# Transposes of q and x: from TensorE to the DMA crossbar on the SyncE queue

## The chip, the cores and the metric

The kernel runs on one core of a Trainium2 chip. The metric is the device time of one execution in microseconds (us). Ratios are the mean time of one kernel's fast runs over the mean of the other's fast runs of the same rounds, so they are not quite the ratio of the medians that stand beside them.

Engine names as in the profile: PE is TensorE (matmuls), PEld its weight loads, DVE is VectorE, ACT is ScalarE, POOL is GpSimd, SP is SyncE. L271 is line 271 of the kernel in question; the changed kernel is 25 lines longer from line 265 on, so L286, L331, L275 of the kernel before are L311, L356, L300 of the changed one.

## The reference

Linear attention followed by a gated feed-forward layer, for 8 batches of 576 tokens, 8 heads of 64.

```python
def _attn_ref(q, k, v, g_norm):
    kv = np.einsum('bhsd,bhse->bhde', k, v)
    out = np.einsum('bhsd,bhde->bhse', q, kv)
    rms = np.sqrt(np.mean(out * out, axis=-1, keepdims=True) + 1e-06)
    return (out / rms * g_norm).astype(np.float32)

def _moe_ref(x, w_gate, w_val, w_out, w_res):      # x: 4608 x 512
    g = x @ w_gate                                  # 512 x 1536
    gelu = 0.5 * g * (1.0 + erf(g * inv_sqrt2))
    val = x @ w_val
    ffn_out = gelu * val @ w_out
    res_gate = 1.0 / (1.0 + np.exp(-(x @ w_res)))
    return (x + res_gate * ffn_out).astype(np.float32)
```

## The kernel before

Each batch has 512 main tokens, a block of its own, and 64 remainder tokens. The remainders of all batches form a ninth block; the remainder rows of two batches are worked on together with the odd one of the pair. The feed-forward part of block b runs on TensorE while the attention of batch b+1 is put between its pieces ("slots"): twelve slots of one gate and one value chain (4 + 4 matmuls of 128x512), then four slots of one residual chain and one output chain (4 + 12 matmuls).

TensorE transposes q (for q times kv) and the normalised x (for the feed-forward part); ACT carries both from PSUM to SBUF, x with the scale g_norm:

```python
def a_qT(b, jj):
    q16 = b16_t[b, "q"].rearrange("p j h d -> p j (h d)")
    ps = pattn.tile([P, 2, NP, P], FP16, tag="at", name="qtp")
    for e in range(2):
        for pr in range(NP):
            nc.tensor.transpose(ps[:, e, pr, :], q16[:, 2 * jj + e, pr * P : (pr + 1) * P], ident)
    nc.scalar.copy(out=st[b]["qT"][:, 2 * jj : 2 * jj + 2, :, :], in_=ps)

def a_xT(b, j):
    ...                                              # cut
    for cc in range(NP):
        nc.tensor.transpose(ps[:, cc, :], t_t[blk][:, jj, cc * P : (cc + 1) * P], ident)
    nc.scalar.activation(out=xT_t[blk][:, :, jj * P : (jj + 1) * P], in_=ps, func=AF.Copy, scale=gcol)

def a_x(b, j):                                       # t*g, for the residual only
    nc.vector.tensor_tensor(out=t_t[blk][:, jj, :], in0=t_t[blk][:, jj, :], in1=g16, op=ALU.mult)
```

The product that closes a slot on DVE, and the chain that reads it:

```python
def m_act(blk, f, gps, vps):
    ge = moep.tile([P, NJ * P], FP16, tag="ge", name="ge")
    nc.scalar.activation(out=ge, in_=gps, func=AF.Gelu)
    nc.vector.tensor_tensor(out=hids[blk][:, f, :], in0=ge, in1=vps, op=ALU.mult)      # hid f
...
    nc.tensor.matmul(fps, lhsT=hids[blk][:, f, j * P : (j + 1) * P], rhs=wo16[:, f, :], ...)
```

The attention plan, one list per slot of the block before (o: q times kv; t: normalised out; x: a_xT; y: a_x):

```python
[by_token q, by_token k],                       # DVE casts q and k to token order
[attn_begin, a_qT(b, 0), load_batch(b + 1)],    # loads of the next batch, issued by POOL
[a_qT(b, 1), a_kv(b, 0, 2)],
[a_kv(b, 2, 4)] + ([a_rem_qT(b)] if odd),
[o[0]] + ([a_rem_o(b)] if odd), [o[1]], [o[2]], [o[3]],
[a_norm(b), t[0], t[1]],                        # slot 8
[t[2], t[3]],
[t[4]] if odd, [],
[x[0], x[1]], [x[2], x[3], y[0], y[1]], [x[4] if odd, y[2], y[3]], [y[4]] if odd
```

(lambdas and slices cut.)

## Time and profile before

| | kernel before |
|---|---|
| time, median of 3 runs | 376.47 us (375.27 to 376.87) |
| span of the profiled run | 373.6 us, granted clock 0.993 |
| PE busy | 358.0 us, 96% |
| a block of the feed-forward part with attention in it (first residual chain of one block to that of the next, 89.06 to 128.14 us) | 39.1 us |

Two more groups of PE work, kept apart by shape, matter later. Columns: line, engine, operation, out<-in, shapes, count; busy us and mean ns; idle time of PE just before them.

```profile
L331 PE MATMUL fps<-wo,hid 128*128 128x512 f16 x432 | 99.6, 379 | 0.0
...
L190 PE MATMUL op<-kv,qT 128*128 128x128 f16 x112 | 10.8, 219 | 0.0
```

PE never stands idle ahead of the output chain (fps) or of q times kv (op): both last columns are 0.0. Those columns show first whether a change has put a wait there.

### The profile page before, as it was taken

To read this page: it belongs to the slowest core of one execution; us is meant where nothing else is said; L and a number is where in the kernel's file an instruction comes from. 1 tells how busy PE (TensorE), PEld (TensorE's weight loads), DVE (VectorE), ACT (ScalarE), POOL (GpSimd) and SP (SyncE) were. 2 spreads that over 40 slices of the span, in tenths; PEclk is the share of its full clock that TensorE was granted. 3 is DMA by queue.
4 is the path that set the end of the run, shared out by engine and by line. 5 is a ranking of instruction groups with operands and counts; after the bars stand their busy time and mean duration, and the time that the engine had idled before them with its cause. 6 is when DMAs were issued, how large, how long until landed. Compare 5 with 4: busy or idle time off the path is not lost.

```text
span 373.6 us, 5442 instructions
## 1 busy us (share of the span) xinstructions
PE 358.0 (96%) x2120; PEld 180.6 (48%) x2120; DVE 215.6 (58%) x427; ACT 153.2 (41%) x257; POOL 47.0 (13%) x65
## 2 busy tenths in 40 slices
PE   6779999999999999999999999999999999999993
PEld 2554464554455455545464445444644444444441
DVE  2566448778546946584657664756478453343422
ACT  3563373453346344544364335533563333123310
POOL 3843140500050002200130005000000000000000
PEclk9899999999999999999999999999999999999998
DMA  9999997590159012901192029601000200020013
GB/s 246 187 202 197 198 200 74 81 221 2 58 107 141 0 56 63 182 5 56 61 172 18 28 84 133 58 31 56 30 0 2 84 29 2 28 80 7 0 43 70
DMA packets 49452, 30.76 MB, mean 82 GB/s; under 512 B 14098, under 2 KB 44818, under 8 KB 49426
## 3 DMA queue, kind: packets, MB, share of 16 engines
q0 software_dynamic: 40848, 17.83, 38.2%
q1 hardware_dynamic: 8578, 12.59, 9.6%
q8 instruction: 16, 0.26, 0.3%
q14 instruction: 10, 0.08, 0.1%
HBM read 38.80 MB, written 9.44 MB: 129 GB/s over the span
## 4 chain that ended last, share of the span: by engine, by line
PE 90%; DVE 5%; DMA 2%; ACT 1%; issue 1%; SPq 0%; DVEq 0%
PE gps L286 25%; PE vps L286 24%; PE fps L331 24%; PE rps L318 8%; DMA qf<-in_q_dram 2%; PE xtp L260 2%; PE kvp L161 2%; PE qtp L151 2%; PE op L190 2%; DVE t L501 1%; DVE pf L337 1%; DVE ss L485 1%; ACT xT L521 1%; PE orp L208 0%; PE kvp L168 0%
## 5 line engine op out<-in xcount | busy, mean ns | idle before, releaser
L286 PE MATMUL gps<-xT,wg 128*128 128x512 f16 (+1 forms) x456 | 112.6, 368 | 2.0 <-ACT xT L521 1.5
L275 DVE TENSOR_TENSOR hid<-ge,vps 128x512 f16<-128x512 f16 x108 | 73.6, 685 | 68.0 <-PE vps L286 67.8
L286 PE MATMUL vps<-xT,wv 128*128 128x512 f16 (+1 forms) x456 | 111.9, 368 | 0.0
L274 ACT ACTIVATE ge<-gps 128x512 f16<-128x512 f32 x108 | 64.5, 598 | 99.7 <-PE gps L286 92.9
L331 PE MATMUL fps<-wo,hid 128*128 128x512 f16 x432 | 99.6, 379 | 0.0
L286 PEld LDWEIGHTS <-wv 128*128 128x128 f16 x456 | 43.6, 98 | 50.2 <-issue 0.2
L331 PEld LDWEIGHTS <-hid 128*128 128x128 f16 x432 | 42.0, 98 | 49.3
L286 PEld LDWEIGHTS <-wg 128*128 128x128 f16 x456 | 41.8, 98 | 42.7 <-issue 2.6
L337 DVE SCALAR_TENSOR_TENSOR pf<-th,fps 128x512 f32<-128x512 f32 x36 | 24.5, 688 | 59.4 <-PE fps L331 59.4
L318 PE MATMUL rps<-wr,xT 128*128 128x512 f16 x144 | 36.9, 379 | 0.1
L327 ACT ACTIVATE th<-rps 128x512 f32<-128x512 f32 x36 | 21.5, 598 | 37.7 <-PE rps L318 37.7
L261 ACT ACTIVATE xT<-xtp,gcol 128x512 f16<-128x512 f16 x32 | 20.5, 685 | 37.6 <-PE xtp L260 37.6
L99 POOL DMA_DIRECT2D qraw<-in_q_dram x7 | 6.3, 894 | 162.0 <-DVE q L106 126.8
L342 DVE SCALAR_TENSOR_TENSOR osb<-pf,t 128x512 f32<-128x512 f32 x36 | 24.9, 691 | 1.1
L184 DVE TENSOR_REDUCE ss<-sq 128x8 f32<-128x512 f32 x32 | 21.9, 686 | 5.5 <-ACT sq L183 3.0
L183 ACT ACTIVATE sq<-op 128x512 f32<-128x512 f32 x28 | 16.8, 598 | 12.0 <-PE op L190 12.0
L318 PEld LDWEIGHTS <-xT 128*128 128x128 f16 x144 | 13.2, 98 | 13.9 <-issue 1.5
L248 DVE TENSOR_TENSOR t<-op,ny 128x512 f16<-128x512 f32 x28 | 17.9, 683 | 0.3
L152 ACT COPY qT<-qtp 128x1024 f16<-128x1024 f16 x14 | 14.2, 1013 | 9.1 <-PE qtp L151 9.1
L161 PE MATMUL kvp<-v,k 128*128 128x128 f16 x128 | 10.9, 222 | 3.3 <-POOL v L434 2.2
L267 DVE TENSOR_TENSOR t<-t,g 128x512 f16<-128x512 f16 x36 | 13.5, 418 | 0.0
L190 PEld LDWEIGHTS <-qT 128*128 128x128 f16 x112 | 8.6, 98 | 6.6
(82 smaller groups left out, 203.4 us busy)
## 6 DMA issues: line engine op xcount, KB each, us to landing
out_dram<-osb SPq DMA_DIRECT2D x32, 256.0 KB, 2.3
qraw<-in_q_dram POOLq DMA_DIRECT2D x7, 512.0 KB, 6.0
kraw<-in_k_dram POOLq DMA_DIRECT2D x7, 512.0 KB, 7.9
v<-in_v_dram POOLq DMA_DIRECT2D x7, 512.0 KB, 9.8
wo<-in_moe_w_out_dram POOLq DMA_DIRECT2D x3, 512.0 KB, 13.8
qf<-in_q_dram SPq DMA_DIRECT2D x2, 512.0 KB, 7.6
kf<-in_k_dram SPq DMA_DIRECT2D x2, 512.0 KB, 6.5
vf<-in_v_dram SPq DMA_DIRECT2D x2, 512.0 KB, 7.8
```

Of the source, the lines that this page charges most:

```text
L161: nc.tensor.matmul(ps, lhsT=k16[:, j, cs], rhs=v16[:, 2 * pr : 2 * pr + 2, j * D : (j + 1) * D], start=(j == 0), stop=False,)
L184: nc.vector.tensor_reduce(out=st[b]["ss"][:, j, :], in_=sq, op=ALU.add, axis=mybir.AxisListType.X)
L248: nc.vector.tensor_tensor(out=t_t[blk][:, jj, :].rearrange("p (h d) -> p h d", h=H), in0=s["o"][j].rearrange("p (h d) -> p h d", h=H), in1 ...
L261: nc.scalar.activation(out=xT_t[blk][:, :, jj * P : (jj + 1) * P], in_=ps, func=AF.Copy, scale=gcol)
L274: nc.scalar.activation(out=ge, in_=gps, func=AF.Gelu)
L275: nc.vector.tensor_tensor(out=hids[blk][:, f, :], in0=ge, in1=vps, op=ALU.mult)
L286: nc.tensor.matmul(ps[:, j0 * P : j1 * P], lhsT=w[:, cc, :], rhs=xT_t[blk][:, cc, j0 * P : j1 * P], start=(cc == 0), stop=(cc == NP - 1),)
L318: nc.tensor.matmul(rps, lhsT=xT_t[blk][:, cc, j * P : (j + 1) * P], rhs=wr16[:, cc, :], start=(cc == 0), stop=(cc == NP - 1),)
L327: nc.scalar.activation(out=th, in_=rps, func=AF.Tanh, scale=0.5)
L331: nc.tensor.matmul(fps, lhsT=hids[blk][:, f, j * P : (j + 1) * P], rhs=wo16[:, f, :], start=(f == 0), stop=(f == NF - 1))
L337: nc.vector.scalar_tensor_tensor(out=pf, in0=th, scalar=1.0, in1=fps, op0=ALU.add, op1=ALU.mult)
L342: nc.vector.scalar_tensor_tensor(out=osb, in0=pf, scalar=0.5, in1=t_t[blk][:, j, :], op0=ALU.mult, op1=ALU.add)
```

## The change

The intent: PE is the bound, so take transposes off it. For batches 2 to 7 the DMA queue of SyncE transposes q (and, in odd batches, the remainder of q) and x from SBUF to SBUF. ACT's copy applied the scale g_norm; the transposing DMA in this kernel carries no scale, so DVE multiplies x with g_norm beforehand. xT is laid out chunk by chunk, so that one DMA can write several of its chunks. As q's transpose takes longer, q times kv and what follows move to one slot later.

```diff
-        xT_t[blk] = pool.tile([P, NP, NJ * P], FP16, ...)
+        xT_t[blk] = pool.tile([P, NJ, NP, P], FP16, ...)
+    def d_qT(b):
+        nc.sync.dma_start(
+            out=st[b]["qT"].rearrange("p j c t -> p (j c) t"),
+            in_=b16_t[b, "q"].rearrange("p j h d -> p (j h d)"),
+            transpose=True,
+        )
+    def d_rem_qT(b):
+        st[b]["qrT"] = attnp.tile([P, NP, P], FP16, tag="qrT", name="qrT")
+        nc.sync.dma_start(out=st[b]["qrT"], in_=qr_t[b // 2], transpose=True)
+    def rem_qT_copy(b):
+        nc.scalar.copy(out=qtr[0][:, :, 0:R], in_=st[b]["qrT"][:, :, 0:R])
+        ...                                          # cut: the other half
+    def d_xT(b, j0, j1):
+        nc.sync.dma_start(out=xT_t[blk][:, k0:k1, :, :]..., in_=t_t[blk][:, k0:k1, :]..., transpose=True)
-                rhs=xT_t[blk][:, cc, j0 * P : j1 * P],
+                rhs=xT_t[blk][:, j0:j1, cc, :],
+    def attn_plan_dma(b):                            # for batches 2 to 7; lambdas cut
+            [by_token q, by_token k],
+            [attn_begin, d_qT(b)] + ([d_rem_qT(b)] if odd) + [load_batch(b + 1)],
+            [a_kv(b, 0, 2)], [a_kv(b, 2, 4)],
+            [rem_qT_copy(b)] if odd,
+            [o[0]] + ([a_rem_o(b)] if odd), [o[1]], [o[2]], [o[3]],
+            [a_norm(b), t[0], t[1], y[0], y[1], d_xT(b, 0, 2)],      # slot 9
+            [t[2], t[3], y[2], y[3], d_xT(b, 2, 4)],
+            [t[4], y[4], d_xT(b, 4, 5)] if odd,
```

(Other places that follow the new layout are cut.)

More of the change, by code (lines that the diff above doesn't have):

```diff
@@ L134, in new_block @@
         t_t[blk] = pool.tile([P, NJ, C], FP16, tag="t" if blk < B else "tl", name="t")
-        xT_t[blk] = pool.tile([P, NP, NJ * P], FP16, tag="xT" if blk < B else "xTl", name="xT")
+        xT_t[blk] = pool.tile([P, NJ, NP, P], FP16, tag="xT" if blk < B else "xTl", name="xT")
     def attn_begin(b):
@@ L261, in a_xT @@
         nc.scalar.activation(
-            out=xT_t[blk][:, :, jj * P : (jj + 1) * P], in_=ps, func=AF.Copy, scale=gcol
+            out=xT_t[blk][:, jj, :, :], in_=ps, func=AF.Copy, scale=gcol
         )
@@ L267, in a_x @@
         nc.vector.tensor_tensor(out=t_t[blk][:, jj, :], in0=t_t[blk][:, jj, :], in1=g16, op=ALU.mult)
+    def d_qT(b):
[9 more added lines that the diff above has]
+        nc.scalar.copy(out=qtr[0][:, :, 0:R], in_=st[b]["qrT"][:, :, 0:R])
+        nc.scalar.copy(out=qtr[1][:, :, R : 2 * R], in_=st[b]["qrT"][:, :, R : 2 * R])
+    def d_xT(b, j0, j1):
+        blk, k0 = where(b, j0)
+        k1 = k0 + j1 - j0
+        nc.sync.dma_start(
+            out=xT_t[blk][:, k0:k1, :, :].rearrange("p j c t -> p (j c) t"),
+            in_=t_t[blk][:, k0:k1, :].rearrange("p j c -> p (j c)"),
+            transpose=True,
+        )
     hids = {}
@@ L319, in m_res @@
                 rps,
-                lhsT=xT_t[blk][:, cc, j * P : (j + 1) * P],
+                lhsT=xT_t[blk][:, j, cc, :],
                 rhs=wr16[:, cc, :],
@@ L516, in f_xT_out @@
         ps = first["xT", half, j0]
-        dst = xT0[:, 2 * half : 2 * half + 2, j0 * P : (j0 + n) * P].rearrange("p c (j t) -> p c j t", j=n)
+        dst = xT0[:, j0 : j0 + n, 2 * half : 2 * half + 2, :].rearrange("p j c t -> p c j t")
         if on_vector:
@@ L631, in attn_plan @@
         ]
+    def attn_plan_dma(b):
+        odd = b % 2 == 1
+        o = [lambda j=j: a_o(b, j) for j in range(NJ)]
+        t = [lambda j=j: a_t(b, j) for j in range(NJ + 1)]
+        y = [lambda j=j: a_x(b, j) for j in range(NJ + 1)]
+        return [
+            [lambda: by_token(b, "q"), lambda: by_token(b, "k")],
+            [lambda: attn_begin(b), lambda: d_qT(b)]
+            + ([lambda: d_rem_qT(b)] if odd else [])
+            + ([lambda: load_batch(b + 1)] if b + 1 < B else []),
+            [lambda: a_kv(b, 0, 2)],
+            [lambda: a_kv(b, 2, 4)],
+            [lambda: rem_qT_copy(b)] if odd else [],
+            [o[0]] + ([lambda: a_rem_o(b)] if odd else []),
+            [o[1]],
+            [o[2]],
+            [o[3]],
+            [lambda: a_norm(b), t[0], t[1], y[0], y[1], lambda: d_xT(b, 0, 2)],
+            [t[2], t[3], y[2], y[3], lambda: d_xT(b, 2, 4)],
+            [t[4], y[4], lambda: d_xT(b, 4, 5)] if odd else [],
+        ]
     late = []
@@ L650 @@
             new_block(blk + 1)
-            for i, fs in enumerate(attn_plan(blk + 1)):
+            for i, fs in enumerate((attn_plan if blk == 0 else attn_plan_dma)(blk + 1)):
                 plan.setdefault((NF - 1 if blk == 0 else 0) + i, []).extend(fs)
```

## The prediction

> **What bounds the kernel now.** I read the page first, its busy times and the chain of waits:
>
> ```profile
> PE 358.0 (96%) x2120; PEld 180.6 (48%) x2120; DVE 215.6 (58%) x427; ACT 153.2 (41%) x257; POOL 47.0 (13%) x65
> ...
> PE 90%; DVE 5%; DMA 2%; ACT 1%; issue 1%; SPq 0%; DVEq 0%
> ```
>
> TensorE (PE) is busy 358.0 of 373.6 us, and 90% of the chain that ends last is PE. So PE time removed shortens the span, unless another engine then makes PE wait. The groups of PE instructions kept apart by shape show what the change can remove:
>
> ```profile
> L260 PE MATMUL xtp<-ident,t 128*128 128x128 f16 x128 | 10.3, 219 | 0.6 <-DVE t L248 0.6
> L151 PE MATMUL qtp<-ident,q 128*128 128x128 f16 x112 | 8.6, 219 | 0.6 <-DVE q L106 0.6
> L200 PE MATMUL qtrp<-ident,qr 128*128 128x128 f16 x16 | 1.5, 219 | 0.0
> ```
>
> The 219 ns is the latency of one transpose; pipelined ones follow faster. The timeline of the block that starts at 103.69 us (block 2, which prepares batch 3) gives the pitch: eight q transposes start at 107.14 and the next gate matmul starts at 107.59, so 56 ns each. Twelve 128x512 matmuls of a chain piece take 2.59 us, so 216 ns each.
>
> The third view is the same timeline where VectorE (DVE) closes the gate/value part (columns: start, length, engine, line):
>
> ```profile
> 121.07 1.03 PE L286 MATMUL gps<-xT,wg 128*128 128x512 f16 x4
> ...
> 123.07 0.69 DVE L275 TENSOR_TENSOR hid<-ge,vps 128x512 f16<-128x512 f16 x1 [0.48 <-PE vps L286]
> ...
> 123.68 0.18 DVE L230 TENSOR_SCALAR nm<-ss 128x40 f32<-128x40 f32 x1
> ...
> 126.21 1.29 DVE L248 TENSOR_TENSOR t<-op,ny 128x512 f16<-128x512 f32 x2
> ...
> 127.41 0.68 DVE L275 TENSOR_TENSOR hid<-ge,vps 128x512 f16<-128x512 f16 x1
> ...
> 128.01 1.28 DVE L248 TENSOR_TENSOR t<-op,ny 128x512 f16<-128x512 f32 x2
> ...
> 129.00 2.75 PE L331 MATMUL fps<-wo,hid 128*128 128x512 f16 x12
> ...
> 129.80 0.68 DVE L248 TENSOR_TENSOR t<-o,ny 128x512 f16<-128x512 f32 x1
> 130.40 0.68 DVE L275 TENSOR_TENSOR hid<-ge,vps 128x512 f16<-128x512 f16 x1
> ```
>
> These hid products are those of slots 8, 9, 10 and 11, the last four of twelve; between them stand the normalisation (nm to ny) and the products t. The first output matmul chain (fps) reads hid of slot 11 only in its twelfth matmul, due at 129.00 + 11 x 0.216 = 131.38. That hid ends at 130.40 + 0.68 = 131.08. So DVE is 58% busy over all, but here it has only 0.3 us of slack before PE would wait.
>
> **What the Trainium skill says.** (1) "VectorE: DVE Perf Modes", section "The three transpose paths": 390 ns for a 128x128 transpose on TensorE, 1309 ns through the DMA crossbar. The trace has 219 ns latency and 56 ns pitch, so on PE a transpose costs less than the page says. (2) "Advanced Engine Details and Errata", section "X-Bar Transpose (TRN2)": transposing DMAs run at 350 to 400 GB/s. The trace of the kernel before has none. (3) "DMA: Bandwidth & Descriptors", section "Anatomy of one DMA": about 2.0 us fixed per DMA. This is given for the software path, but the 256 KB output stores, issued by SyncE, landing in 2.3 us, fit it. (4) The same page, section "Issuing engines are not separate DMA queues": all queues share the 16 DMA engines. In the trace the loads of the next batch fill these from 109.8 to 118.3 us, just when a q transpose would run.
>
> **The change part by part.** *Removed from PE:* for batches 2 to 7, 16 q and 16 x transposes each, and in batches 3, 5, 7 four more of each for the remainder rows: 6 x 32 + 3 x 8 = 216. At 56 ns: 12.1 us, all on the path. That alone would be 3.2% of 376.47. *Removed from ScalarE (ACT):* 12 qT copies at 1.01 us and 27 scaled xT copies at 0.69 us, some 31 us, but ACT is 41% busy and waits for PE: worth nothing by itself. *New xT layout:* the gate/value matmuls now read four runs of 128 columns. The matmuls of k and v already read two runs of 64 columns at 222 ns against 219 for others, so I count it as free.
>
> *Moved on DVE, which I hold for the main point.* The order of instructions in the changed kernel shows the normalisation one slot later (after hid 9, not hid 8), and the products t*g, formerly done near the end of the block, now between hid 9, hid 10 and hid 11. Count from T, the start of slot 9's gate matmuls. In the trace the slot 8 hid starts 2.00 after its slot's start (123.07 - 121.07) and the norm 2.61 after. The norm takes 2.53 (123.68 to 126.21), each t or hid 0.60 (pitch in the rows above), a pair of t*g about 0.67 (two ran in 0.75 at the block's end, overlap taken off). So norm from T+2.61; two t from T+5.14; two t*g from T+6.34; hid 10 from T+7.01; two t from T+7.61; two t*g from T+8.81; hid 11 from T+9.48 to T+10.16. PE: three slots of eight matmuls at 0.216 (5.19), four rps (0.86), eleven fps (2.38): it wants hid 11 at T+8.43. **PE waits 1.73 us**, with the restart some 1.8, in each of six blocks: 10.8 us. hid 10 is ready at T+7.69, in time for the tenth product's turn at T+8.21. So the twelve us removed come nearly all back as one wait per block.
>
> *Added on the DMA queue.* One transpose of 128x2048 f16 (512 KB) for q per batch, two of 256 KB for x, and 128 KB for each remainder. For x: t*g of the second pair ends at T+9.5, and the next block begins at about T+5.19 + 4 x 3.46 + 1.8 = T+20.8, so it has 11 us: hidden. For q: its cast ended at 106.98, that is 3.3 us into the block. The first o matmul now comes after six slots and 20 k-v matmuls: 6 x 1.73 + 20 x 0.056 = 11.5 us. **The budget is 8.2 us.** Estimate: 2.0 fixed and 0.52 MB at 350 GB/s 1.5 make 3.5 us alone. But it splits into short rows, shares the engines with the loads from about 2.8 us after its start, and the 1309 ns of the page for one 128x128 block, times 16 blocks one after another, would be 21 us. I choose 8.5 us as the middle, wide: a wait of 0.3 us in each of six blocks, 2 us.
>
> *Sum:* 376.5 - 12.1 + 10.8 + 2 = 377, and as the q transfer can be late by much but not early by much, I put the time at **378 us**.
>
> **The rivals.** (a) *All transposes hidden, PE's time simply falls.* For: PE at 96%, the 12.1 us are real, ACT and the PSUM banks get freer. Against: the DVE count above. It would give 376.5 - 12.1 = 364. (b) *The DVE wait alone, transfers hidden.* For: the 8.2 us budget is over twice the 3.5 us estimate. It gives 375. (c) *The q transpose comes late.* For: the loads keep all 16 engines full 2.8 us after the cast, the rows are short, and the author already moved o by one slot. Each us beyond 8.2 costs 6 us: landing after 10 us gives 386, after 12 us 398. In odd blocks ACT's remainder copies stand in order ahead of the next gelu and would hold it too. Against: the queue has the engines to itself for 2.8 us. (d) *The transposes delay output stores in the same SyncE queue.* Against: the stores wait mostly for DVE now, and come after the x transposes with PE work of 3.46 us between two of them.
>
> **Range and chances.** 364 needs the DVE count to be wrong; I give faster by over 2% (under 369) 0.12. Between 369 and 384 the DVE wait holds and the q transpose lands within about 9.4 us: 0.50. Above 384: 0.38, since I have no duration for such a transpose from this chip's traces. Range for 8 in 10: 368 to 402.
>
> **What would show it.** PE loses 216 transposes and about 12 us of summed pitch. In each block 1 to 6 the twelfth fps matmul of the first output chain should stand idle 1.5 to 2 us for DVE's hid; if it is under 0.5 us, my DVE count is wrong. If the first op matmul waits for the qT transpose, its landing time minus 8.2 should be that wait. The gate matmuls of a new block should not wait for xT. If the 128x512 matmuls got longer than 216 ns in pitch, the layout was not free. The prediction fails if the q transposes take far over 10 us, or if DVE gets the t*g done in gaps that I did not see.

## The result, and the profile after

| | before | after |
|---|---|---|
| time, median | 375.87 us (4 runs) | 400.93 us (400.28 to 401.73, 4 runs) |
| ratio | | 1.0665, 95% interval 1.063 to 1.0699 |
| span, granted clock of the profiled run | 373.6 us, 0.993 | 399.2 us, 0.963 |
| PE busy, instructions | 358.0 us, 2120 | 353.9 us, 1904 |

The changed kernel is slower by about 25 us. PE has 216 instructions fewer, as counted, and yet its share of the span fell from 96% to 89%: it waits. First the page of the changed kernel: engines, granted clock of PE over 40 slices (tenths), and the chain that ended last.

```profile
PE 353.9 (89%) x1904; PEld 170.7 (43%) x1904; DVE 215.7 (54%) x427; ACT 126.0 (32%) x218; POOL 46.8 (12%) x65
...
PEclk9889999959999699999998999999999999999998
...
PE 68%; DVE 15%; DMA 13%; issue 2%; ACT 1%; SPq 0%; POOL 0%; DVEq 0%
```

The chain, formerly 90% PE, now runs through DVE (15%) and DMA (13%). The clock falls in three slices in the middle of the work (5, 6 and 8), which it did not do before. The waits of PE in order of size (columns: total us, times, longest):

```profile
PE op L190 <- DMA qT<-q: 15.4, 4, 9.5
...
PE fps L356 <- DVE hid L300: 9.5, 6, 1.6
...
PE orp L208 <- ACT qtr L282: 5.3, 2, 2.8
```

Here are both waits that the prediction named: q times kv (op) for the DMA of qT, and the output chain (fps) for DVE's hid, six times. The third is new: orp, the q times kv of the remainder rows, waits for ACT, and ACT for the DMA of the remainder's transpose.

**The wait for hid**, in the timeline of block 1 of the changed kernel (start, length, engine, line; in brackets the idle time before):

```profile
100.14 2.54 PE L356 MATMUL fps<-wo,hid 128*128 128x512 f16 x11
...
100.35 0.75 DVE L267 TENSOR_TENSOR t<-t,g 128x512 f16<-128x512 f16 x2
...
101.02 0.68 DVE L300 TENSOR_TENSOR hid<-ge,vps 128x512 f16<-128x512 f16 x1
...
101.62 1.28 DVE L248 TENSOR_TENSOR t<-op,ny 128x512 f16<-128x512 f32 x2
102.82 0.75 DVE L267 TENSOR_TENSOR t<-t,g 128x512 f16<-128x512 f16 x2
...
103.49 0.68 DVE L300 TENSOR_TENSOR hid<-ge,vps 128x512 f16<-128x512 f16 x1
...
104.22 0.39 PE L356 MATMUL fps<-wo,hid 128*128 128x512 f16 x1 [1.55 <-DVE hid L300]
```

Eleven matmuls of the first output chain run, the twelfth stands 1.55 us for hid 11, which ends at 103.49 + 0.68 = 104.17. The t*g products now stand ahead of it on DVE. In odd batches the wait is 1.63 us.

**The wait for q** in block 2 of the changed kernel, where batch 3 is prepared:

```profile
118.25 4.09 SPq L271 DMA_TRANSPOSE qT<-q  x1
...
118.39 0.89 POOL L99 DMA_DIRECT2D qraw<-in_q_dram  x1 [44.37 <-DVE q L106]
...
122.45 1.32 SPq L279 DMA_TRANSPOSE qrT<-qr  x1
...
128.99 0.40 PE L190 MATMUL op<-kv,qT 128*128 128x128 f16 x4 [2.54 <-DMA qT<-q]
...
131.74 0.40 ACT L282 COPY qtr<-qrT 128x256 f16<-128x256 f16 x1 [7.25 <-DMA qrT<-qr]
...
132.20 1.23 PE L208 MATMUL orp<-kv,qtr 128*128 128x128 f16 x8 [2.81 <-ACT qtr L282]
...
133.22 1.91 PE L311 MATMUL gps<-xT,wg 128*128 128x512 f16 x4
```

SyncE issues the q transpose at 118.25; at 118.39 POOL begins to issue the loads of the next batch, since both wait for the same cast of q on DVE. The transpose lands 10.7 us after its issue; the remainder's, issued behind it at 122.45, lands 9.3 us after its own issue, and ACT's copies wait for it. The last row shows a third cost: these four matmuls span 1.91 us where the same group spanned 1.03 us before. The clock that was granted had fallen.

The landing times of the six q transposes, against the moment when the loads start beside them:

| batch | loads start, relative to the transpose's issue | landing, us after issue | PE waits at op (and orp), us |
|---|---|---|---|
| 2 | 2.0 us ahead | 14.9 | 9.5 |
| 3 | 0.14 after | 10.7 | 2.5 (2.8) |
| 4 | 0.66 after | 6.8 | none |
| 5 | 0.23 after | 9.9 | 1.6 (2.5) |
| 6 | 0.23 after | 10.0 | 1.8 |
| 7 | no loads | 4.4 | none |

For batch 2 the transpose also stood in SyncE's queue behind two output stores of block 0, at 71.3 us where the cast had ended at about 69. The first thought is contention: alone the transpose takes 4.4 us. A 3 us window (80 to 83 us) of block 1 shows how the engines are shared (columns: queue, packets, MB, share of 16 engines; q0 are the loads, q1 is SyncE's queue):

```profile
q0 software_dynamic: 718, 0.36, 87.7%
q1 hardware_dynamic: 717, 0.18, 46.8%
```

In this window, which is batch 2's, both queues send equally many packets. A load packet carries 0.36 MB / 718, about 500 bytes written, one of the transpose about 250. The Trainium skill says in "DMA: Bandwidth & Descriptors", section "Queues, rings and completion order", that each DMA engine goes round between queues at packet granularity; 717 against 718 agrees, if a record of the trace is a packet of the page, which no run shows. At that rate, 239 packets per us, a transpose of 512 KB in rows of 256 bytes (2048 packets, an estimate from the size) takes 8.6 us.

Equal turns do not explain the other batches. In batch 6 the transpose sent 1747 of its packets from 248.5 to 252.5 us, before the first packet of the loads. (It was slow even then: 1095 packets from 250.5 to 252.5 us, while POOL was issuing the loads, against 1688 in 2 us of batch 7.) What followed from 253.0 to 257.5 us:

```profile
q0 software_dynamic: 1573, 0.80, 140.4%
q1 hardware_dynamic: 98, 0.02, 4.0%
```

Its last 98 packets were spread over 4.5 us beside 1573 of the loads, and it landed at 258.5. Why these last packets take so long is not shown.

### The profile page after: what moved, and what is told of

It is laid out like the page before. It is cut to its first block, busy times and chain, and to the rows that moved or that the text cites. A ratio compares the mean times of both kernels' runs of the same rounds, so it can differ in the third digit from the quotient of the medians.

```text
span 399.2 us, 5027 instructions
## 1 busy us (share of the span) xinstructions
PE 353.9 (89%) x1904; PEld 170.7 (43%) x1904; DVE 215.7 (54%) x427; ACT 126.0 (32%) x218; POOL 46.8 (12%) x65
## 4 chain that ended last, share of the span: by engine, by line
PE 68%; DVE 15%; DMA 13%; issue 2%; ACT 1%; SPq 0%; POOL 0%; DVEq 0%
PE gps L311 19%; PE fps L356 19%; PE vps L311 18%; PE rps L343 6%; DMA qT<-q 6%; DMA qrT<-qr 5%; DVE t L248 4%; DVE hid L300 3%; DMA vf<-in_v_dram 2%; PE op L190 2%; DVE t L267 1%; PE kvp L161 1%; DVE na L237 1%; DVE ny L238 1%; DVE na L236 1%
## 5 line engine op out<-in xcount | busy, mean ns | idle before, releaser
L311 PE MATMUL gps<-xT,wg 128*128 128x512 f16 (+1 forms) x456 | 116.3, 378 | 1.7 <-ACT xT L546 1.3
L311 PE MATMUL vps<-xT,wv 128*128 128x512 f16 (+1 forms) x456 | 114.4, 375 | 0.0
L311 PEld LDWEIGHTS <-wv 128*128 128x128 f16 x456 | 44.8, 100 | 51.9 <-issue 3.2
L311 PEld LDWEIGHTS <-wg 128*128 128x128 f16 x456 | 43.4, 101 | 45.1 <-issue 4.3
L352 ACT ACTIVATE th<-rps 128x512 f32<-128x512 f32 x36 | 21.5, 598 | 89.9 <-PE rps L343 89.9
L184 DVE TENSOR_REDUCE ss<-sq 128x8 f32<-128x512 f32 x32 | 21.8, 685 | 17.4 <-ACT sq L183 15.4
L190 PE MATMUL op<-kv,qT 128*128 128x128 f16 x112 | 11.3, 226 | 15.4 <-DMA qT<-q 15.4
L343 PEld LDWEIGHTS <-xT 128*128 128x128 f16 x144 | 13.9, 98 | 15.7 <-DMA wr<-in_moe_w_res_dram 0.4
L161 PEld LDWEIGHTS <-k 128*128 128x128 f16 x128 | 9.0, 98 | 6.7 <-issue 3.5
```

What stands on the lines that cost most here:

```text
L161: nc.tensor.matmul(ps, lhsT=k16[:, j, cs], rhs=v16[:, 2 * pr : 2 * pr + 2, j * D : (j + 1) * D], start=(j == 0), stop=False,)
L184: nc.vector.tensor_reduce(out=st[b]["ss"][:, j, :], in_=sq, op=ALU.add, axis=mybir.AxisListType.X)
L190: nc.tensor.matmul(ps[:, pr * P : (pr + 1) * P], lhsT=s["qT"][:, j, pr, :], rhs=s["kv2"][:, pr, :], start=True, stop=True)
L311: nc.tensor.matmul(ps[:, j0 * P : j1 * P], lhsT=w[:, cc, :], rhs=xT_t[blk][:, j0:j1, cc, :], start=(cc == 0), stop=(cc == NP - 1),)
L343: nc.tensor.matmul(rps, lhsT=xT_t[blk][:, j, cc, :], rhs=wr16[:, cc, :], start=(cc == 0), stop=(cc == NP - 1),)
L352: nc.scalar.activation(out=th, in_=rps, func=AF.Tanh, scale=0.5)
```

## The experiments

Theory: (1) 216 transposes off PE are worth 12.1 us; (2) the hid wait costs 9.5 us; (3) the q transposes are late only since they share the engines with the loads, and PE's waits for them cost 20.7 us (15.4 + 5.3); (4) the rest, 399.2 - (373.6 - 12.1 + 9.5 + 20.7) = 7.5 us, is the clock that falls in those waits. Rivals: the crossbar or its issue is slow in itself; the new layout slows the matmuls; the clock costs nothing of its own.

| run | edit | median, us | ratio to the kernel before, 95% interval |
|---|---|---|---|
| e1_layout | new xT layout alone | 374.99 | 1.0012 (0.9975 to 1.0049) |
| e2_loads_late | loads placed after slot 6 | 400.89 | 1.0691 (1.0669 to 1.0714) |
| e3_hid_first | t*g and the second pair of t behind hid 11 | 391.80 | 1.0441 (1.0425 to 1.0457) |
| e4_both | e2 and e3 | 391.77 | 1.0440 (1.0414 to 1.0465) |
| e5_x_only | x by DMA, q on PE | 372.25 | 0.9903 (0.9877 to 0.9929) |
| e6_loads_late_o_early | e2, o one slot earlier | 407.27 | 1.0844 (1.0806 to 1.0882) |
| e7_fill | idle matmuls in the q waits | 395.11 | 1.0527 (1.0495 to 1.0559) |
| e8_loads_slot3 | loads placed after slot 3 | 400.55 | 1.0667 (1.0639 to 1.0695) |
| e9_gate | loads wait for qT | 372.89 | 0.9930 (0.9903 to 0.9956) |
| e10_gate_hid | e9 and e3 | 362.61 | 0.9651 (0.9626 to 0.9677) |
| e11_x_only_behind | e5, t*g behind hid 11 | 369.02 | 0.9843 (0.9814 to 0.9873) |

All gave correct results. The kernel before measured 375.2 to 375.6 us (medians) beside them.

### e1: the layout alone

```diff
-            for i, fs in enumerate((attn_plan if blk == 0 else attn_plan_dma)(blk + 1)):
+            for i, fs in enumerate(attn_plan(blk + 1)):
```

> Only the xT layout of the change (chunk by chunk), all transposes back on TensorE as in the kernel before. Theory (layout free): 375.9 us within 1, the same 216 ns pitch of the 128x512 matmuls. Rival (reading four runs of 128 columns slows the 848 gate/value matmuls): every 5 ns of pitch more would cost 4 us, so 380 or more.

374.99 us, ratio 1.0012. The gate and value matmuls measure 379 ns each, as before. Reading four runs of 128 columns costs nothing that can be seen here; this rival falls.

### e2 and e8: loads placed later in the program

```diff
             [attn_begin, d_qT(b)] + ([d_rem_qT(b)] if odd)
-            + ([load_batch(b + 1)] if b + 1 < B else []),
...
-            [o[1]],
+            [o[1]] + ([load_batch(b + 1)] if b + 1 < B else []),     # e8: after a_kv(b, 2, 4)
```

> The changed kernel with the loads of the next batch issued after slot 6 instead of slot 1, so that the q transpose has the DMA engines to itself. Theory (contention with the loads): the q transpose lands after 4.4 us in each block, as it did for batch 7 which has no loads beside it; the waits of op and orp (20.7 us) and the half clock after them (about 7 us) go, the wait for hid (9.5 us) stays: about 373 us. Rival (the transpose itself, or its issue on SyncE, is slow): it still lands after some 10 us and the time stays near 401 us.

> As e2, but the loads come after slot 3: some 4 us after the cast of q instead of 9. Theory (the transpose only needs 4.4 us of the engines for itself): as e2, within 2 us. Rival (what counts is that the loads stay away for the whole budget of 8.2 us): 3 us or more above e2.

Both missed: 400.89 and 400.55 us, op still waits 15.1 and 14.2 us. That looks like the rival's win, but the trace shows that the edit did not do what it was meant to do. Rows of e2:

```profile
118.31 3.71 SPq L271 DMA_TRANSPOSE qT<-q  x1
```

```profile
118.45 0.89 POOL L99 DMA_DIRECT2D qraw<-in_q_dram  x1 [44.61 <-DVE q L106]
```

The loads still start 0.14 us after the transpose. POOL has a program of its own and does little but issue loads; it waits only for the cast that frees the raw buffer. A later place in the source changes nothing when the issuing engine has nothing else to pass. These two runs say nothing about contention.

### e3 and e4: the order on DVE

```diff
-            [a_norm(b), t[0], t[1], y[0], y[1], d_xT(b, 0, 2)],
-            [t[2], t[3], y[2], y[3], d_xT(b, 2, 4)],
+            [a_norm(b), t[0], t[1]],
+            [],
+            [y[0], y[1], d_xT(b, 0, 2), t[2], t[3], y[2], y[3], d_xT(b, 2, 4)],
             [t[4], y[4], d_xT(b, 4, 5)] if odd,
```

> The changed kernel with the t*g products, the second pair of t and the x transposes moved behind hid 11 on VectorE; nothing else. Theory: the 1.6 us wait of the twelfth fps matmul for hid goes in all six blocks, 9.5 us less: 391 us. Rival (the time lost there is swallowed by another wait, as x lands later and the output evacuations come later): about 400 us.

> Both edits together. Theory: only the removed 216 transposes are left over, 375.9 - 12.1 = 363.8 us. Rival (a third cost in the transposes, such as slower matmuls or DMA beside them): 367 us or more.

e3 gives 391.80 us, 9.1 us less than the changed kernel, and no wait of fps for hid is left. (The edit moves t[2] and t[3] too, so the gain is not that of t*g alone.) x is transposed later now, and no gate chain waits for it. e4 was to add the late loads, which were not late; it equals e3 (391.77 us), and says nothing more.

### e5 and e11: x alone

The edit puts a_qT, a_rem_qT and o back in their old slots, and keeps the DMA transposes of x.

> Only x goes through the DMA queue (q back on TensorE, loads in their old place, hid 11 ahead of the t*g products). 108 transposes leave TensorE: 6.0 us. Theory: the x transposes are hidden, no wait in their place: 369.9 us. Rival (crossbar transposes cost by themselves, whatever they carry): 374 us or more.

372.25 us, against 369.9 of theory. The trace has six waits of 0.34 us for hid, 2.0 us in sum. The order of instructions showed why: with o one slot earlier the whole tail had moved up by one slot, so that the t*g products stood between hid 10 and hid 11. The expectation described another kernel than the one that ran. e11 puts one empty slot in:

```diff
             [a_norm(b), t[0], t[1]],
             [],
+            [],
             [y[0], y[1], d_xT(b, 0, 2), t[2], t[3], y[2], y[3], d_xT(b, 2, 4)],
```

> e5 mended: in e5 the t*g products stood between hid 10 and hid 11, not behind hid 11 as its expectation said, and six waits of 0.34 us for hid were left. Here they stand behind hid 11. Theory: no wait is left, 108 transposes fewer at 56 ns, 375.5 - 6.0 = 369.5 us. Rival (crossbar transposes of x cost something beside the waits): 372 us as e5.

369.02 us, 6.2 us below the kernel before (375.22 us): the whole worth of 108 transposes at 56 ns. The transposes of x hide completely.

### e6: o one slot earlier

```diff
-            [rem_qT_copy(b)] if odd,
-            [o[0]] + ([a_rem_o(b)] if odd),
+            ([rem_qT_copy(b)] if odd) + [o[0]] + ([a_rem_o(b)] if odd),
```

> Loads late as in e2, and o back in slot 4, so that the normalisation stands behind hid 8 again; the t*g products stay between hid 9, 10 and 11. By the count of the prediction hid 11 is then ready at about the time when the twelfth fps matmul wants it: wait 0 to 0.2 us per block, 364 to 365 us. Rival (the added t*g products are the whole cause of the hid wait, not the shift by a slot): the wait of about 1.5 us stays, 373 us.

407.27 us. The loads were not late here either, so the shorter budget made q's waits longer: 24.7 us at op. But the run does tell what made the hid wait: it fell from 1.55 to 0.21 us in even batches. In odd ones it is 1.27 us, as there the remainder's t and t*g come ahead of hid 11 again. So the wait came of two things together, the shift by one slot and the t*g products moved forward: taking back the first removes most of it in even batches, and moving t*g and two t behind hid 11 (e3) removes all of it. The shift also gave the transpose of q its time: without it the waits at op grew from 15.4 to 24.7 us.

### e7: the clock

```diff
+    WARM_O = {2: 34, 3: 8, 4: 0, 5: 4, 6: 4, 7: 0}       # idle matmuls ahead of o[0], by batch
+    WARM_R = {3: 10, 5: 8, 7: 0}                          # and ahead of a_rem_o
```

> The changed kernel with idle matmuls on zeros put where TensorE waits for q or qr (34 in block 1, 8 + 10 in block 2, 4 + 8 in block 4, 4 in block 5), fewer than the waits are long. Theory (the waits let the granted clock fall to half for some us after them): the clock stays near 1.0 and the time falls by 4 to 7 us, to 394 to 397 us, though more work is done. Rival (the clock is not a cost of its own): 401 us or more.

395.11 us, 5.8 us less than the changed kernel with 68 matmuls more; the granted clock of its runs is 0.984 to 0.990 against 0.963 to 0.972. So the fallen clock is a cost of its own. Its size can be estimated: PE worked some 12 us at half the clock in the changed kernel (86.3 to 89.9, 132.2 to 137.7 and 216.4 to 219.6 us, mean granted clock 0.51), which cost about 6 us. In e7 one drop is left, after a wait of 3.2 us in block 1: some 3.4 us at half the clock (87.5 to 91.5 us, mean 0.57), about 1.7 us. So the clock accounts for some 4.3 of the 5.8 us; the rest lies partly in waits that were slightly shorter (4.6 us with 15.7 us of idle matmuls, against 20.7). Of the 7.5 us that the theory gave to the clock, 1.5 are not accounted for. How it falls shows in the windows of the changed kernel in block 1, where PE stood from about 76.8 to 86.3 us (columns: window, then busy us and count of PE, PEld, DVE, ACT, POOL; PEclk, DMA share, GB/s):

```profile
78.00:80.00 2.00, 0.00 (x0) 0.00 (x0) 0.00 (x0) 0.00 (x0) 0.00 (x0) 0.90 1.30 176
86.00:88.00 2.00, 1.73 (x8) 0.90 (x9) 0.45 (x1) 0.60 (x1) 0.00 (x0) 0.50 1.59 232
88.00:90.00 2.00, 2.00 (x7) 0.74 (x6) 0.24 (x1) 0.60 (x1) 0.00 (x0) 0.54 0.03 2
90.00:92.00 2.00, 2.00 (x15) 1.06 (x14) 1.37 (x2) 1.19 (x2) 0.00 (x0) 1.00 0.00 0
```

Here the clock drops to half some 3 us into the wait and comes back some 3.5 us after work has resumed (in blocks 2 and 4 some 5.4 and 3.1 us after): 7 instructions are seen between 88 and 90 us, 15 in the next 2 us. The Trainium skill warns of this in "TensorE: Matmul & The Clock Gate", section "Why this matters for your kernels": no idle gaps over about 3 us. In this trace the waits of 1.55 us (hid) and 1.8 us (batch 6) left the clock alone; two waits close together, such as 1.63 and 2.45 us for batch 5, did not.

### e9 and e10: loads that wait for the transpose

```diff
+    gate_t = consts.tile([1, 1], FP16, name="gate_t")
+    def gate(b):
+        nc.gpsimd.tensor_copy(out=gate_t, in_=st[b]["qT"][0:1, 0, 0, 0:1])
...
-            + ([load_batch(b + 1)] if b + 1 < B else []),
+            + ([gate(b), load_batch(b + 1)] if b + 1 < B else []),
```

POOL copies one element of qT, and so issues the loads only when the transpose has landed. e10 adds the edit of e3.

> e2 and e8 missed: GpSimd, which issues the loads, waits for nothing but the cast of q, so a later place in the program did not delay them. Here GpSimd first copies one element of qT, so the loads of the next batch start only when the q transpose has landed; nothing else differs from the changed kernel. Theory (contention): the q transpose lands 4.4 us after its issue in every block, the waits of op and orp (20.7 us) go, the clock returns to 0.99, the hid wait (9.5 us) stays: 373 us. Rival (the transpose is slow in itself, batch 7 being special): landing near 10 us, time 400 us or more.

> The gate of e9 and the VectorE order of e3 together. Theory: no wait takes the place of the 216 transposes, 375.5 - 12.1 = 363 to 364 us, faster than both kernels by 3% and more. Rival (a third cost): 367 us or more.

e9 gives 372.89 us, as the theory said to 0.1 us. Its landing times of qT, and its largest wait of PE:

```profile
DMA to landing us min/median/max: 4.3/4.4/5.0
```

```profile
PE fps L356 <- DVE hid L300: 9.5, 6, 1.6
PE kvp L161 <- POOL v L459: 2.0, 1, 2.0
```

Every q transpose lands after 4.3 to 5.0 us, in place of 4.4 to 14.9; no wait for q or the remainder is left, and the clock is back at 0.993. The hid wait stands alone and has its old size. Delaying the loads by some 5 us cost nothing, as they are needed a block later. In batch 2 the transpose still stands behind the two stores (issue at 70.6 us, against 71.3), and yet it lands in time. The gate holds back both the issuing of the loads on POOL and their packets, so the run shows that the loads are the cause, but not by which of the two.

e10 gives 362.61 us, 3.5% faster than the kernel before and 9.6% faster than the changed one. Its page, and its two largest waits of PE:

```profile
PE 346.2 (96%) x1904; PEld 168.8 (47%) x1904; DVE 215.5 (60%) x427; ACT 125.5 (35%) x218; POOL 47.7 (13%) x70
```

```profile
PE kvp L161 <- POOL v L459: 2.6, 1, 2.6
PE gps L311 <- ACT xT L546: 1.5, 3, 0.6
```

PE is at 96% again, with 216 instructions less; both waits belong to the start of the kernel, which the change does not touch. The span fell by 373.6 - 360.8 = 12.8 us. e10 has more on the DMA engines than the kernel before and is bound by PE all the same.

## Why the prediction was right or wrong

The measured 400.93 us lies inside the range, near its upper end; "within 2%" had the largest chance and "slower", which came, 0.38. The range held it by its width, not by the sum, which missed by 23 us. Step by step:

- **216 transposes at 56 ns, 12.1 us: right.** e10 leaves a span 12.8 us shorter, e11 shows 6.2 us for half of them.
- **ACT's saved work worth nothing, layout free: right.** ACT's busy time fell from 153.2 to 126.0 us in a kernel that got slower, and e10's gain is explained by PE's transposes alone; e1 measured 1.0012.
- **The DVE wait of 1.73 us, with the restart 1.8, in six blocks, 10.8 us: right**, slightly too large. The trace has 1.55 to 1.63 us, 9.5 us in sum; e3 gained 9.1 and e10 over e9 10.3 us. That count was made from durations and the order of instructions alone, and DVE ran in the order that it assumed. (A slip without effect: hid 10 is read by the eleventh product, not the tenth; its time, T+8.21, is right.)
- **x hidden with 11 us to spare: right.** It landed 2.7 us after issue.
- **q's transpose: the term that was mis-sized.** The prediction put the middle landing at 8.5 us against a budget of 8.2, and so 2 us for all six blocks. The budget held: a landing after 6.8 us left no wait, one after 9.9 us a wait of 1.6. But the median landing was 10.0 us and the longest 14.9, and the waits for q came to 15.4 us at op, 20.7 with the remainder. Three parts of the step failed. Alone the transpose took 4.4 us, not 3.5. A head start on the loads did not save it: batch 6 had 4.0 us without a packet of theirs, more than the 2.8 that were assumed, and landed after 10.0 all the same, while batch 2 came 2.0 us *after* the loads, held up behind output stores. And it took one middle for six transposes: a wait grows only above the budget, so the spread costs more than the middle tells. (A slip in the chances: by the prediction's own sum, 384 us stands for a landing after 9.7 us, not 9.4.)
- **The remainder's transpose had no term.** It landed 9.3 and 10.1 us after its issue in the two odd batches in which loads ran, and ACT's copies, which wait for it, let orp wait 5.3 us of the 20.7. The third rival named those copies as a risk, without a size.
- **A term was missing: the clock.** The prediction counted waits as time lost once. The waits for q also halved the clock after them; 7.5 us by difference, about 6 by the windows of the trace, of which e7 won back some 4.3.
- **The rival "transposes delay stores in SyncE's queue"** came true both ways in block 1: two stores delayed the transpose of batch 2, and the other two, whose data were ready by 74.2 us, were issued behind it at 78.7. PE waited for none of these stores.

In sum the prediction had 12.1 - 10.8 - 2 and the runs had 12.1 - 9.5 - 20.7 - 7.5, which makes 25.6 us more (the last term is a difference, so that the sum must close). The third rival, "the q transpose comes late", was the right one, and its own figure (386 us for a landing after 10 us) was too low for want of the clock, the remainder and the spread.

## What to carry to other kernels

When work moves from a full engine to a DMA, give the transfer its time on the shared queues as carefully as its time on the path: here the loads that the same event set free arrived at just that moment, and a transfer of 4.4 us took 6.8 to 14.9. To delay such loads, make their issuing engine wait for something; a later place in the source does nothing for an engine that has no other work. And look at the order on the engine that is *not* the bound: t*g products that moved up by a few places in six blocks took back most of the twelve us that the change had freed, and moving them behind one product gave it back.

## What the Trainium skill lacked or had wrong

- "VectorE: DVE Perf Modes" gives 390 ns for a TensorE transpose of 128x128. In this trace one has a latency of 219 ns, and eight in a row follow each other every 56 ns, which is what counts for a full engine.
- "Advanced Engine Details and Errata" gives 350 to 400 GB/s for crossbar transposes. Here, from SBUF to SBUF with no loads beside them, the DMA view shows 215 GB/s while q is transposed (290 to 292 us) and 289 GB/s while x is (102.45 to 103.15 us). With the time to issue and to land, 256 KB took 2.7 us and 512 KB 4.4.
- No page says what a transpose costs beside loads. Here 512 KB landed after 6.8 to 14.9 us with 1.5 MB of loads beside it. Its packets are half as large as those of the loads; in one stretch the two took equal turns (717 to 718), in another its last 98 packets went beside 1573 of the loads.
- "DMA: Bandwidth & Descriptors" calls the sequencer's issue time usually small. A 512 KB transpose held SyncE's queue 1.8 us with the engines free, and up to 7.3 us beside loads.
